# A pooled attention and token/channel mixer on one core: feature-half head, three score bursts, contiguous uT, column-tiled tails

## The chip, the cores and the metric

The kernel runs on 1 core of one Trainium2 chip. The metric is the device time of one execution in microseconds. Shown is the median of the runs with its lowest and highest value.

## What is computed

For 8 batches of 8 heads, 576 positions and 64 features, K and V are averaged over groups of 8 positions (72 pooled keys), attention is taken over the 72 keys, and the result x (8, 576, 512) goes through a token mixer and a channel mixer:

```python
k_p = k.reshape(B, H, Sp, pool, D).mean(axis=3)            # Sp = 72, pool = 8
v_p = v.reshape(B, H, Sp, pool, D).mean(axis=3)
attn = softmax(scale * np.matmul(q, k_p.transpose(0, 1, 3, 2)))
attn_out = np.matmul(attn, v_p)                            # (8, 8, 576, 64)
x = attn_out.transpose(0, 2, 1, 3).reshape(B, S, H * D)    # (8, 576, 512)
h = np.maximum(x.transpose(0, 2, 1) @ w_tok1, 0.0) @ w_tok2  # 576 -> 256 -> 576
u = x + h.transpose(0, 2, 1)
out = u + np.maximum(u @ w_ch1, 0.0) @ w_ch2               # 512 -> 1536 -> 512
```

Inputs and output are float32. The kernel works in bfloat16 with float32 accumulation.

## The kernel before

**Positions.** A batch's 576 positions are cut into 4 chunks of 128 and a tail of 64 (c = 0 to 3 and c = 4). The tails of two batches share one 128-row tile, and all 8 tails are the last MLP unit.

**Order of the work.** Nothing is scheduled automatically: each engine runs its instructions in the order in which the program issues them, and waits for its semaphores at the head of its queue. The order is written out by hand. `HEAD` is a list of steps for batch 0's attention and token mixer (d8 is eight dummy matmuls on a zeroed tile). Then come units 0 to 8: unit n is the channel MLP of batch n (unit 8: of all tails). A unit is a Python generator which yields every two or four matmuls, 45 to 48 times. `PLAN[n]` says which steps of later batches are issued after which yield: "15: 1.K0 1.Q0" issues two steps of batch 1 after yield 15 of that unit.

**Steps of a batch.** `lk lq lv` start the loads, by DMAs on POOL's queue that cast to bfloat16. `K0 K1 V0 V1` pool on POOL by three adds a half (L164 to L170), `k0 .. v1` do the same on VectorE, `kp vpool` on TensorE by eight accumulating identity matmuls. `kpT` transposes the pooled keys, `Q0 Q1` transpose q on VectorE (L262). `s0` to `s3` are score bursts: 8 matmuls with 32 contraction rows each on four row tiles of TensorE (L273), then two exponentials on ACT (L279). `av` is attention times V with the sum in a 65th column (L311), divided on VectorE (L323, L329). `at0 at1` are the first token product (L357) with its relu, `u` the second (L372) with the residual added on VectorE (L373). For the tails, w_tok2's last 64 columns lie in a zero-padded tile `w_tok2t`, so that two batches' tails add up into one 128-row output by four full matmuls.

**u transposed.** The MLP needs u with features on the partitions. Batches 0 to 3 transpose it on TensorE (`t`, L382) and copy it out on VectorE (L383). Batches 4 to 7 write u to device memory (`M0 M2 M4`, L391), read it back in 32-row pieces (`M`, L398, SP's queue) and transpose 32x32 blocks of 4-byte pairs on VectorE (`T`, L405). Such a uT holds pairs of features side by side, and L467 reads every second element of it.

**The MLP.** Twelve tiles of four matmuls each (L467) and relu on ACT into GT (L471). Unit 0 then does twelve matmuls for each chunk (L494, added out in L500). Units 1 to 8 form the 512x512 second product by seven half-size products (L543, 12 matmuls of 256 columns each). This needs sums of GT tiles on VectorE (`=1a` to `=4b`, L514 and L521) and sums of w_ch2, which are formed once on VectorE at the start of unit 1 (L514). Products go to a PSUM bank as two contiguous halves `ps[:, i]` and are added out on VectorE (`plus`, L564) into s or into o, which SP stores.

**Gates.** `g` makes POOL wait for VectorE's place in its queue (L623, L624).

PSUM has four one-bank buffers (`ps_one`) and two two-bank buffers (`ps_two`, for scores and av).

Of the kernel before, what the change touches and what calls it, by code (L numbers as in the profile page):

```python
# [8 lines left out]
FP32 = mybir.dt.float32  # L9
# [11 lines left out]
HEAD = """c0 c1 d8 q0 d1 q1 d5 kp0 kp1 kt0 d2 o0 e0 kt1 kp2 kp3 o1 e1 kt2 kt3 q2 q3 d2 o2 e2 vpool0 o3 d1 vpool1 e3 d2  # L21
          aw1 av0 av2 d2 av3 at_0 at_2 av4 at_1 at_3 d2 at_4 X0 X1 X2 A0 A1 A2 X3 A3 d3"""
PLAN = [
    {0: "0.u0", 2: "0.u3", 6: "1.k1", 10: "2.lv", 15: "1.K0 1.Q0", 16: "1.kpT 1.Q1 3.lk", 18: "1.V0 1.s1 0.u2", 20: "1.s0", 22: "3.lq 1.v1 1.s2", 24: "2.K0 1.s3", 25: "1.av1", 26: "1.av4", 27: "0.u1 1.av3 1.av2", 30: "2.K1", 32: "1.av0", 36: "1.at0 1.at1", 38: "1.u3 2.V0", 40: "1.u4 1.u0", 44: "3.lv 1.u2 1.u1", 45: "1.t3 1.t0", 46: "1.t1", 47: "1.t2 1.t4"},
    {4: "g", 7: "3.K0 2.kpT", 8: "2.Q1", 9: "2.Q0", 11: "2.s2", 12: "3.Q0", 13: "3.Q1", 14: "2.v1 =3a 2.s0", 15: "4.lv 4.lk", 16: "2.s1", 17: "=1a", 18: "2.s3 =3b", 19: "2.av1", 20: "2.av3", 21: "2.av2", 22: "4.lq", 23: "3.K1 2.av0", 24: "2.av4", 26: "g", 27: "=1b", 28: "3.kpT =2a", 29: "2.at0", 30: "3.s3", 31: "=2b", 32: "=4b 2.at1 =4a", 34: "3.s2", 36: "2.u2", 38: "3.V0", 39: "2.u0 3.s1 2.u3", 40: "2.t2", 41: "2.u1 2.t3", 42: "3.s0 3.V1 2.t0 2.t1"},
    {0: "4.K0 3.av4 5.lk 5.lq", 2: "3.av3", 4: "4.K1", 6: "3.av0", 9: "3.av2", 10: "4.V0 3.av1", 12: "=3b", 14: "3.at0 3.at1", 15: "=3a", 16: "4.kpT", 17: "g", 18: "4.Q0", 19: "=1a 3.u3 4.s1", 20: "4.Q1", 23: "3.u1 4.s3 =2a", 24: "3.u0 =1b 3.u2", 25: "=2b 3.t1", 26: "4.s0", 28: "3.u4 4.s2 =4b", 29: "4.V1", 30: "=4a g", 33: "3.t0", 34: "3.t2 4.av3", 35: "3.t3", 37: "4.av4", 39: "3.t4 4.av1", 41: "5.lv", 42: "4.av2", 44: "4.av0"},
    {0: "5.Q0", 6: "=3a 5.K0", 7: "4.at0 4.at1", 8: "5.K1 5.kpT", 9: "5.V0 4.u1 4.u0 5.Q1", 10: "4.u3 5.s1", 11: "5.V1", 12: "4.u2", 13: "5.s0", 14: "4.M0", 15: "4.M2", 16: "4.M", 17: "5.s3 6.lk", 18: "=3b", 20: "=1a", 21: "g", 22: "5.av3 =2a", 23: "=1b", 24: "6.lq", 25: "=2b", 27: "5.s2 =4a", 28: "=4b", 31: "g 5.av2", 36: "5.av4", 38: "4.T1 4.T3", 39: "4.T2", 40: "4.T0", 43: "5.av0", 44: "5.av1 6.lv"},
    {0: "6.Q0", 6: "=3a 6.K0", 7: "5.at0 5.at1", 8: "6.K1 6.kpT", 9: "6.V0 5.u1 5.u0 6.Q1", 10: "5.u3 6.s1", 11: "6.V1 5.u4", 12: "5.u2", 13: "6.s0", 14: "5.M0", 15: "5.M4 5.M2", 16: "5.M", 17: "6.s3 7.lk", 18: "=3b", 20: "=1a", 21: "g", 22: "6.av3 =2a", 23: "=1b", 24: "7.lq", 25: "=2b", 27: "6.s2 =4a", 28: "=4b", 31: "g 6.av2", 36: "6.av4", 38: "5.T1 5.T3", 39: "5.T2", 40: "5.T0", 43: "6.av0", 44: "6.av1 7.lv 5.T4"},
    {0: "7.Q0", 6: "=3a 7.K0", 7: "6.at0 6.at1", 8: "7.K1 7.kpT", 9: "7.V0 6.u1 6.u0 7.Q1", 10: "6.u3 7.s1", 11: "7.V1", 12: "6.u2", 13: "7.s0", 14: "6.M0", 15: "6.M2", 16: "6.M", 17: "7.s3", 18: "=3b", 20: "=1a", 21: "g", 22: "7.av3 =2a", 23: "=1b", 25: "=2b", 27: "7.s2 =4a", 28: "=4b", 31: "g 7.av2", 36: "7.av4", 38: "6.T1 6.T3", 39: "6.T2", 40: "6.T0", 43: "7.av0", 44: "7.av1"},
    {6: "=3a", 7: "7.at0 7.at1", 9: "7.u1 7.u0", 10: "7.u3", 11: "7.u4", 12: "7.u2", 14: "7.M0", 15: "7.M4 7.M2", 16: "7.M", 18: "=3b", 20: "=1a", 21: "g", 22: "=2a", 23: "=1b", 25: "=2b", 27: "=4a", 28: "=4b", 31: "g", 38: "7.T1 7.T3", 39: "7.T2", 40: "7.T0", 44: "7.T4"},  # L30
    {6: "=3a", 18: "=3b", 20: "=1a", 21: "g", 22: "=2a", 23: "=1b", 25: "=2b", 27: "=4a", 28: "=4b", 31: "g"},
    {14: "=3b", 22: "=1a", 24: "=2a =1b", 25: "=4a", 28: "=2b", 31: "=4b", 34: "=3a"},
# [4 lines left out]
def kernel(  # L37
# [14 lines left out]
    nc = tc.nc  # L52
    B, H, S, D = q.shape
    P = 128
    POOL = 8
    SP = S // POOL
# [3 lines left out]
    SH = S // 2  # L60
# [21 lines left out]
    w_tok2t = singles.tile([P, 2, 2, P], BF16)  # L82
# [8 lines left out]
    u_tails = singles.tile([P, 4, DM], BF16)  # L91
    area = early.tile([P, 6 * 1024], BF16, name="area")
    kpz = area[0:SP, 0:2048].rearrange("j (h e d) -> j h e d", h=H, e=4)
# [9 lines left out]

    def kv(t, src, b, h0, h1, j0=0, j1=SP):
        nc.gpsimd.dma_start(out=t[j0:j1, h0:h1].rearrange("j h i d -> j h (i d)"),
                            in_=src[b, h0:h1].rearrange("h (j i) d -> j h (i d)", i=POOL)[j0:j1])

    def load_kv(b, src, key):
        t = loaded[b, key] = raw.tile([SP, H, POOL, D], BF16, name=key + "r")
        if b == 0:  # L110
            for h0, h1, j0, j1 in ((0, HP, 0, BP), (0, H, BP, SP), (HP, H, 0, BP)):
                kv(t, src, b, h0, h1, j0, j1)
        else:
            kv(t, src, b, 0, H)

    def load_q(b):
        qb = loaded[b, "q"] = raw.tile([P, HP, BR * D + D], BF16, name="qb")
        if b == 0:
            nc.vector.memset(qb[:, :, BR * D:], 0.0)
            nc.gpsimd.dma_start(out=qb[:, 2:HP, 0:BR * D], in_=q_pairs(2, HP))  # L120
        else:
            nc.gpsimd.dma_start(out=quarters(qb), in_=q[b].rearrange("(g l) (j n) d -> (l j) g (n d)", l=4, n=2 * BR))
# [8 lines left out]
    def load_tok():  # L131
        nc.gpsimd.dma_start(out=f2, in_=moe_w_tok2.rearrange("(c p) n -> p c n", p=P))
# [9 lines left out]
    def permute_tok2():  # L142
        src = f2.rearrange("t m (p r) -> t m r p", r=BR)
        dst = w_tok2.rearrange("t m (r p) -> t m r p", p=BP)
        for m in range(2):
            nc.gpsimd.tensor_copy(out=dst[:, m], in_=src[:, m])
        for half in range(2):
            nc.gpsimd.tensor_copy(out=w_tok2t[:, :, half, half * BP:(half + 1) * BP], in_=w_tok2[:, :, 8 * BP:S])

    def load_ch1():  # L150
        for g in range(3):
            cols = slice(g * 512, (g + 1) * 512)
            nc.gpsimd.dma_start(out=w_ch1[:, :, cols], in_=moe_w_ch1[:, cols].rearrange("(p c) n -> p c n", c=4))
# [17 lines left out]

    tails = {}

    def batch_steps(b):
# [5 lines left out]
        def prepare():  # L180
            kp = kpz if first else att.tile([SP, 2, 2, 4, D // 2], BF16, name="kp")
# [12 lines left out]
        def late(key):  # L194
            if key not in st:
                pool, shape = {"x": (mix, [P, 4, DM]), "u": (mix, [P, 4, DM]), "uT": (mix, [P, 4, 4 * P]),
                               "AT": (att, [P, 2, DM]), "qD": (att, [P, 2, S, 2])}[key]
                st[key] = pool.tile(shape, BF16, name=key)
            return st[key]

        def parts(src):
            return src.rearrange("p (m k) -> p k m", k=4)
# [14 lines left out]
        def kp2(a):  # L217
            def go():
                ps = ps_one.tile([P, 512], FP32, name="p1")
                hs = slice(2 * a, 2 * a + 2)  # L220
                for i in range(POOL):
                    nc.tensor.matmul(out=ps[0:SP, 0:2 * D], lhsT=ident[0:SP, 0:SP], rhs=loaded[b, "k"][:, hs, i, :],
                                     start=(i == 0), stop=(i == POOL - 1))
                view = ps[0:SP, 0:2 * D].rearrange("j (h d) -> j h d", d=D)[:, :, None, :].broadcast_to([SP, 2, 2, D])
                (nc.scalar.copy if a == 1 else nc.vector.tensor_copy)(out=kpz[:, hs, 0:4:3, :], in_=view)
            return go

        def kt2(a):
            def go():
                ps = ps_one.tile([P, 2, 2, SP], BF16, name="p1")  # L230
                for odd in range(2):
                    for hl in range(2):
                        nc.tensor.transpose(out=ps[:, odd, hl, :],
                                            in_=kpz[:, 2 * a + hl, 2 * odd:2 * odd + 2].rearrange("j e d -> j (e d)"),
                                            identity=ident[0:SP, 0:SP])
                nc.vector.tensor_copy(out=kT[:, :, 2 * a * SP:(2 * a + 2) * SP], in_=ps.rearrange("m o h j -> m o (h j)"))
            return go

# [28 lines left out]
        def score4(g, half):  # L267
            def go():
                pss = [ps_two.tile([P, 2, 512], FP32, name="p2") for _ in range(2)]
                for db in range(2):  # L270
                    for l in range(4):
                        quad = slice(l * 32, (l + 1) * 32)
                        nc.tensor.matmul(out=pss[l // 2][0:SP, l % 2, 0:SH], lhsT=st["kD"][quad, g, db, :],  # L273
                                         rhs=st["qD"][quad, g, half * SH:(half + 1) * SH, db],
                                         start=(db == 0), stop=(db == 1), tile_position=(l * 32, 0))
                exv = st["ex"][:, 0:H * S].rearrange("j (h n) -> j h n", h=H)[:, :, half * SH:(half + 1) * SH]
                for a in range(2):
                    h = 4 * g + 2 * a
# [426 lines left out]
```

## Time and profile before

| | |
|---|---|
| median of 3 runs | 276.22 us (275.23 to 276.26) |
| profiled execution | 277.01 us, span from first to last instruction 275.2 us |
| granted TensorE clock | 1.0 |
| instructions | 5195 |
| TensorE (PE) busy | 262.3 us, 95% of the span |
| weight loads (PEld) | 156.8 us, 57% |
| VectorE (DVE) | 192.2 us, 70% |
| ScalarE (ACT) | 113.5 us, 41% |
| GpSimd (POOL) | 144.8 us, 53% |
| DMA | 32.71 MB in 36344 packets |

Busy time is the union of an engine's instructions. Matmuls are pipelined, so that a row's mean duration of one matmul (383 ns for 512 columns) is longer than the distance between two of them. The idle time of an engine which nothing waits for costs nothing.

### The profile page before, as it was taken

The page shows a single profiled execution, that of the slowest core. Times are in us where ns is not written, and L with a number is a line of the kernel's source. Part 1 is how long each engine was busy: PE and PEld are TensorE (multiplying, and loading weights), DVE is VectorE, ACT ScalarE, POOL GpSimd, SP SyncE. Part 2 cuts the span into 40 slices and gives each one's busy share as a digit, 9 for nine tenths or more (in the row PEclk, how much of TensorE's full clock was granted, in tenths as well). Part 3 has the DMA queues.
Part 4 walks back from the last instruction along what each step waited for, and adds up shares of the span by engine and source line. Part 5 has one row for each costly group of instructions (what it writes and reads, how often), then busy time and mean ns, then how long its engine had stood idle before and what let it go on. Part 6 is the DMA issues. An engine that isn't in the chain of part 4 may idle for free.

```text
span 275.2 us, 5195 instructions
## 1 busy us (share of the span) xinstructions
PE 262.3 (95%) x2064; PEld 156.8 (57%) x2092; DVE 192.2 (70%) x378; ACT 113.5 (41%) x200; POOL 144.8 (53%) x138
## 2 busy tenths in 40 slices
PE   8989889989999999999997999999999999999994
PEld 3765335454466654784376436944594477477483
DVE  5455887389999978896586765795595568174273
ACT  2453672107834357306840566046604430621610
POOL 8595693974989996199619971798000000010000
PEclk9999999999999999999999999999999999999999
DMA  7999999928491591065399539972405250402204
GB/s 160 188 202 207 203 204 195 193 69 161 65 173 26 101 206 20 4 97 144 90 168 152 155 69 172 176 169 89 88 2 152 86 107 18 136 2 59 96 0 152
DMA packets 36344, 32.71 MB, mean 119 GB/s; under 512 B 13665, under 2 KB 29921, under 8 KB 36321
## 3 DMA queue, kind: packets, MB, share of 16 engines
q0 software_dynamic: 18672, 17.64, 41.9%
q1 hardware_dynamic: 17376, 14.49, 20.7%
q8 instruction: 16, 0.26, 0.4%
q10 hardware_dynamic: 272, 0.26, 0.3%
q14 instruction: 8, 0.06, 0.1%
HBM read 38.21 MB, written 11.80 MB: 182 GB/s over the span
## 4 chain that ended last, share of the span: by engine, by line
PE 58%; DMA 18%; DVE 14%; POOL 4%; issue 2%; ACT 2%; SPq 1%; DVEq 0%; POOLq 0%; ACTq 0%
PE p L467 23%; PE p L543 18%; DMA v<-mem 7%; PE p L372 5%; DMA kr<-in_k_dram 5%; PE p L357 5%; DVE area L514 4%; DMA mem<-u 3%; DMA area<-in_moe_w_tok_dram 3%; PE p L494 3%; PE p L311 2%; PE p L273 2%; DVE u L373 1%; DVE x L329 1%; DVE qD L262 1%
## 5 line engine op out<-in xcount | busy, mean ns | idle before, releaser
L471 ACT ACTIVATE GT<-p 128x512 bf16<-128x512 f32 x108 | 64.4, 596 | 98.9 <-PE p L467 58.3
L467 PE MATMUL p<-uT,w_ch 128*128 128x512 bf16 x366 | 91.8, 383 | 3.4 <-DVE uT L405 1.9
L467 PEld LDWEIGHTS <-w_ch 128*128 128x128 bf16 x432 | 39.4, 97 | 49.5 <-issue 6.5
L624 POOL COPY flag<-flag 1x1 f32<-1x1 f32 x14 | 3.5, 247 | 82.2 <-DVE flag L623 82.2
L279 ACT ACTIVATE ex<-p 72x576 bf16<-72x576 f32 x56 | 33.0, 641 | 18.0 <-PE p L273 17.9
L543 PEld LDWEIGHTS <-area 128*128 128x128 bf16 x384 | 36.6, 98 | 5.2 <-issue 0.5
L543 PE MATMUL p<-area,area 128*128 128x256 bf16 x288 | 36.2, 273 | 0.0
L165 POOL TENSOR_TENSOR t<-t 72x512 f32<-72x512 f32 x25 | 34.3, 1372 | 2.0
L373 DVE TENSOR_TENSOR u<-p,x 128x512 bf16<-128x512 f32 x32 | 21.5, 684 | 13.4 <-PE p L372 13.3
L543 PEld LDWEIGHTS <-GT 128*128 128x128 bf16 x288 | 27.1, 98 | 6.2 <-issue 1.4
L164 POOL TENSOR_TENSOR t<-kr 72x1024 f32<-72x1024 bf16 x13 | 27.7, 2129 | 5.0 <-DMA kr<-in_k_dram 4.6
L164 POOL TENSOR_TENSOR t<-vr 72x1024 f32<-72x1024 bf16 x12 | 25.7, 2143 | 0.7
L543 PE MATMUL p<-w_ch,GT 128*128 128x256 bf16 x192 | 23.8, 273 | 0.1
L564 DVE TENSOR_TENSOR o<-p,s 128x512 f32<-128x512 f32 (+1 forms) x32 | 20.6, 664 | 2.6 <-PE p L543 2.5
L521 DVE TENSOR_TENSOR area<-GT 128x768 bf16<-128x768 bf16 x16 | 10.3, 641 | 16.8 <-ACT GT L471 16.7
L329 DVE TENSOR_TENSOR x<-p,den 128x512 bf16<-128x512 f32 x30 | 20.7, 692 | 1.0
L564 DVE TENSOR_TENSOR s<-p,u 128x512 f32<-128x512 f32 x28 | 19.2, 685 | 3.2 <-PE p L543 3.1
L514 DVE TENSOR_TENSOR area<-GT 128x768 bf16<-128x768 bf16 x16 | 12.7, 798 | 9.6 <-ACT GT L471 9.6
L311 PEld LDWEIGHTS <-ex 72*128 72x128 bf16 x320 | 14.9, 98 | 7.1 <-DVE x L329 1.3
L372 PE MATMUL p<-AT,w_tok 128*128 128x512 bf16 x63 | 17.8, 379 | 0.4 <-DVE u L373 0.4
L311 PE MATMUL p<-vp,ex 72*128 72x65 bf16 x320 | 16.8, 194 | 1.1 <-DVE x L329 0.3
L348 ACT ACTIVATE AT<-p 128x512 bf16<-128x512 f32 x15 | 9.0, 597 | 20.8 <-PE p L357 18.1
(102 smaller groups left out, 325.0 us busy)
## 6 DMA issues: line engine op xcount, KB each, us to landing
out_dram<-o SPq DMA_DIRECT2D x33, 256.0 KB, 3.5
kr<-in_k_dram POOLq DMA_DIRECT2D x7, 576.0 KB, 11.1
qb<-in_q_dram POOLq DMA_DIRECT2D x7, 576.0 KB, 12.1
vr<-in_v_dram POOLq DMA_DIRECT2D x7, 576.0 KB, 8.8
w_ch<-in_moe_w_ch_dram POOLq DMA_DIRECT2D x6, 512.0 KB, 13.3
mem<-u SPq DMA_DIRECT2D x8, 256.0 KB, 2.1
v<-mem SPq DMA_DIRECT2D x8, 160.0 KB, 5.1
v<-mem SPq DMA_DIRECT2D x8, 128.0 KB, 5.4
```

Source lines behind the costliest of these rows:

```text
L164: eng.tensor_tensor(out=t4[:, 0:n], in0=t[:, hs, 0:4], in1=t[:, hs, 4:8], op=ALU.add)
L165: eng.tensor_tensor(out=t4[:, 0:n, 0:2], in0=t4[:, 0:n, 0:2], in1=t4[:, 0:n, 2:4], op=ALU.add)
L279: nc.scalar.activation(out=exv[:, h:h + 2], in_=pss[a][0:SP, :, 0:SH], func=AF.Exp, scale=scale)
L311: nc.tensor.matmul(out=halves[h // 4][:, (h % 4) * (D + 1):(h % 4 + 1) * (D + 1)], lhsT=st["ex"][:, h * S + n0:h * S + n0 + P], rhs=st["vp ...
L329: nc.vector.tensor_tensor(out=dst.rearrange("p (a h d) -> p a h d", a=2, d=D), in0=view[:, :, :, 0:D], in1=den[rows, :, :, None].broadcast ...
L372: nc.tensor.matmul(out=ps, lhsT=w, rhs=a, start=(i == 0), stop=(i == len(mms) - 1))
L373: nc.vector.tensor_tensor(out=dst, in0=ps, in1=x, op=ALU.add)
L467: nc.tensor.matmul(out=ps, lhsT=w_ch1[:, kk, m * P:(m + 1) * P], rhs=uT[kk], start=(kk == 0), stop=(kk == 3))
L471: nc.scalar.activation(out=GT[:, m, :], in_=ps, func=AF.Relu)
L514: nc.vector.tensor_tensor(out=out, in0=a, in1=b, op=ALU.subtract)
L543: nc.tensor.matmul(out=ps[i] if split else ps[:, i], lhsT=a(m)[:, i * P:(i + 1) * P], rhs=w(m), start=start and m == 0 and (i == 0 or spli ...
L564: nc.vector.tensor_tensor(out=out[:, i], in0=ps[i] if type(ps) is list else ps[:, i], in1=other[:, i], op=ALU.add)
```

## The change

**Head.** K, V and the weights are loaded in a new order by `L..` steps; w_ch1 comes in four pieces. `a02` and its like (`avh`) make av of two chunks for four heads, `m02` and its like (`ath`) the first token product of a chunk for half of the features, its relu half on ACT and half on VectorE. w_tok2 is permuted on ACT and VectorE instead of POOL. **Scores.** Two bursts of 8x384 columns, one for each four heads, and one of 16x192 for the rest of all heads. **Batch 1** is pooled on TensorE (`kpool`, `vpool`). **K and V loads** are two DMAs each, 64 rows and 8 rows. **Tails.** `w_tok2t` goes; each batch's tail product writes 64 output rows at column position 0 or 64. The tails' transposes go through memory (`M4`, `MT`, `T4`, `T5`). **u and uT.** u holds two chunks interleaved element by element; the pieces read back are 256 elements wide, and the 4-byte pairs are pairs of positions, so that uT is contiguous and GT's columns are taken with step 2 instead (`chunk`). A product writes every second element of its PSUM bank, `ps[:, :, i]`, and `plus` works on pairs. **Weight sums** are eight steps `w0` to `w7` inside unit 0. All plans are rewritten; below are HEAD and, as an example, units 3 and 4.

```diff
-HEAD = """c0 c1 d8 q0 d1 q1 d5 kp0 kp1 kt0 d2 o0 e0 kt1 kp2 kp3 o1 e1 kt2 kt3 q2 q3 d2 o2 e2 vpool0 o3 d1 vpool1 e3 d2
-          aw1 av0 av2 d2 av3 at_0 at_2 av4 at_1 at_3 d2 at_4 X0 X1 X2 A0 A1 A2 X3 A3 d3"""
+HEAD = """LkA LkT LkB Lq LvT LvA LvB Lt1 Lt2 Lv1 Lc1a Lc1b Lk1 Lc1c Lq1 Lc1d Lc2b Lc2a Lc2c d6 d6 prep c0 d1 d3 q0 d4 c1 d4 kp0 q1 kt0 kp1 e0 kt1 kp2 o0 q2 o1 kt2 e1 q3 o2 vpool0 o3 d1 a02 e2 vpool1 a00 e3 d1 m02 m03 a04 m00 a10 p0 X1 m04 a12 X0 m01 m10 p1 a14 m11 m13 m12 A0 X2 m14 A1 X3 A2 A3"""
...
+    {0: "0.u2 0.u3 g 1.vpool1", 2: "2.lk 0.u0", 4: "1.vpool0 2.lq", 7: "1.kpool 1.Q0", 9: "1.kpT 2.lv", 12: "1.s0", 15: "1.Q1", 18: "1.s2", 19: "0.u1", 20: "w4", 21: "w0", 22: "1.s1", 25: "1.av4 w2", 26: "3.lk 3.lq", 27: "1.av3 w1", 29: "1.av0", 30: "2.K0", 31: "1.av1", 32: "1.av2", 33: "2.Q0 w5", 34: "1.at0", 35: "2.K1 1.at1 1.u4", 36: "1.u2", 37: "2.Q1 1.u3", 38: "1.t2", 40: "1.u0", 41: "1.u1 1.t0", 43: "1.t1", 44: "2.kpT", 46: "1.t3", 47: "w7 w3 w6 2.s0"},
...
-    {0: "5.Q0", 6: "=3a 5.K0", 7: "4.at0 4.at1", 8: "5.K1 5.kpT", 9: "5.V0 4.u1 4.u0 5.Q1", 10: "4.u3 5.s1", 11: "5.V1", 12: "4.u2", 13: "5.s0", 14: "4.M0", 15: "4.M2", 16: "4.M", 17: "5.s3 6.lk", 18: "=3b", 20: "=1a", 21: "g", 22: "5.av3 =2a", 23: "=1b", 24: "6.lq", 25: "=2b", 27: "5.s2 =4a", 28: "=4b", 31: "g 5.av2", 36: "5.av4", 38: "4.T1 4.T3", 39: "4.T2", 40: "4.T0", 43: "5.av0", 44: "5.av1 6.lv"},
+    {1: "4.av0 3.T4", 2: "6.lk", 4: "6.lq 5.K1", 6: "4.av3 5.K0", 7: "4.at0", 8: "4.at1 =3a", 11: "5.kpT =3b", 12: "4.u2 5.s0", 13: "5.V0", 15: "4.u3", 16: "5.s1 4.u0", 18: "4.u1", 19: "5.V1", 20: "=1a g", 21: "g", 22: "3.T5 5.av2", 24: "4.M2 =2a =4a g", 26: "5.s2", 28: "4.M0 =1b =2b", 29: "4.M", 30: "4.T1", 31: "g", 32: "=4b", 34: "4.T0", 35: "5.av0", 36: "4.T2 5.av1", 40: "4.T3 5.av3", 44: "6.lv 6.Q1 5.av4"},
...
     def load_kv(b, src, key):
         t = loaded[b, key] = raw.tile([SP, H, POOL, D], BF16, name=key + "r")
...
-            kv(t, src, b, 0, H)
+        kv(t, src, b, 0, H, 0, BP)
+        kv(t, src, b, 0, H, BP, SP)
...
+        def scores(i):
+            def go():
+                pss = [ps_two.tile([P, 2, 512], FP32, name="p2") for _ in range(2)]
+                spans = [(i, 0, 0, S1)] if i < 2 else [(g, g * (S - S1), S1, S) for g in range(2)]
+                for g, o, n0, n1 in spans:
+                    for db in range(2):
+                        for l in range(4):
+                            quad = slice(l * 32, (l + 1) * 32)
+                            nc.tensor.matmul(out=pss[l // 2][0:SP, l % 2, o:o + n1 - n0], lhsT=st["kD"][quad, g, db, :],
+                                             rhs=st["qD"][quad, g, n0:n1, db], start=(db == 0 and o == 0),
+                                             stop=(db == 1), tile_position=(l * 32, 0), skip_group_check=True)
...
-                    mms = [(w_tok2t[:, m, half, :], tails[b // 2, half][:, m, :]) for half in range(2) for m in range(2)]
+                    for m in range(2):
+                        for half in range(2):
+                            nc.tensor.matmul(out=ps[half * BP:(half + 1) * BP], lhsT=w_tok2[:, m, 8 * BP:S],
+                                             rhs=tails[b // 2, half][:, m, :], start=(m == 0), stop=(m == 1),
+                                             tile_position=(0, half * BP), skip_group_check=True)
...
+    def chunk(u, c, a):
+        return a[:, c::2] if "paired" in u else a[:, c * P:(c + 1) * P]
...
-                    nc.tensor.matmul(out=ps[i] if split else ps[:, i], lhsT=a(m)[:, i * P:(i + 1) * P], rhs=w(m),
+                    nc.tensor.matmul(out=ps[i] if split else ps[:, :, i], lhsT=chunk(u, i, a(m)), rhs=w(m),
...
-            return ps_one.tile([P, 2, 256], FP32, name="p1")
+            return ps_one.tile([P, 256, 2], FP32, name="p1")
...
+        def cols_of(o, half):
+            r = o[:, :, half * 256:(half + 1) * 256]
+            return lambda e: r[:, e] if type(e) is int else r.rearrange("p i n -> p n i")
```

## The prediction

> **What bounds the kernel now.** I read the page first, then the busy times by stretch, then TensorE's timeline, its waits, and the chain of waits. The page says TensorE, but its busy time counts overlapped matmuls, so it can't say how much is left to gain.
>
> ```profile
> PE 262.3 (95%) x2064; PEld 156.8 (57%) x2092; DVE 192.2 (70%) x378; ACT 113.5 (41%) x200; POOL 144.8 (53%) x138
> ...
> PE 58%; DMA 18%; DVE 14%; POOL 4%; issue 2%; ACT 2%; SPq 1%; DVEq 0%; POOLq 0%; ACTq 0%
> ```
>
> The kernel is a head (batch 0's attention), units 0 to 7 (the channel MLP of batch n, with attention and token mixing of later batches woven in) and unit 8 (all tails). A unit begins at its first matmul of L467. Busy time by unit:
>
> ```profile
> 0.00:25.20 25.20, 22.89 (x200) 14.48 (x204) 14.01 (x41) 10.54 (x22) 19.11 (x33) 1.00 1.12 187
> 25.20:60.05 34.85, 32.41 (x218) 15.22 (x221) 24.27 (x35) 12.76 (x23) 25.51 (x20) 1.00 1.11 184
> 60.05:92.50 32.45, 30.91 (x277) 17.81 (x280) 31.59 (x56) 17.02 (x30) 26.37 (x22) 1.00 0.57 94
> 92.50:122.80 30.30, 30.02 (x288) 19.26 (x290) 26.11 (x52) 12.92 (x23) 21.46 (x18) 1.00 0.52 91
> ...
> 149.60:179.40 29.80, 28.09 (x234) 16.75 (x234) 20.90 (x46) 12.52 (x22) 20.12 (x18) 1.00 0.77 141
> ```
>
> Columns: stretch, length, then busy time of PE, weight load, DVE, ACT and POOL, granted clock, DMA share, GB/s. Unit 1 has DVE at 31.6 of 32.45 us: there VectorE binds. Elsewhere it is TensorE, and what counts is its spacing:
>
> ```profile
> 78.87 0.59 PE L357 MATMUL p<-x,w_tok 128*128 128x512 bf16 x2
> 79.30 0.38 PE L357 MATMUL p<-xt,w_tok 128*128 128x512 bf16 x1
> 79.51 0.60 PE L543 MATMUL p<-area,area 128*128 128x256 bf16 x4
> 80.04 0.45 PE L273 MATMUL p<-qD,kD 32*72 32x288 bf16 x8
> 80.43 1.05 PE L543 MATMUL p<-area,area 128*128 128x256 bf16 x8
> ```
>
> Two matmuls of 512 columns start 0.43 us apart: 0.2155 each. Of 256 columns it is 0.109 (84 of L543 in 9.17 us of the chain), of 128 it is 0.055, of 65 it is 0.033. The four of L543 should end at 79.95; the score burst starts at 80.04, and 0.39 later the next work starts. So a burst costs 0.48: two groups of four row tiles side by side, 0.24 of stream, and 0.24 around it (0.09 on either side, the rest between groups).
>
> With these prices I count each unit's matmuls into a need. Unit 1: 48 L467 10.35, 84 L543 9.14, 8 bursts 3.8, 10 L357 2.16, 8 L372 1.72, 40 L311 1.28, transposes 1.15: 29.6. Likewise head 19.2, unit 0 31.6, unit 2 29.9, 3 26.7, 4 27.5, 5 26.7, 6 24.2, 7 and 8 19.5 each: 254.4. Lengths less needs are losses: head 6.0, then 3.3, 2.9, 0.4, 0.1, 2.3, 1.1, 0.4, 0.5, and 3.9 for the last adds and stores: 20.8, with the needs 275.2. Only about 11 of them lie in units 0 to 7. TensorE's waits name the largest (total, times, longest):
>
> ```profile
> PE p L467 <- DVE uT L405: 1.9, 2, 1.5
> PE p L213 <- POOL kp L168: 1.7, 1, 1.7
> PE p L467 <- DVE uT L383: 0.7, 1, 0.7
> ```
>
> And on the chain of waits (start, length, what):
>
> ```profile
> 34.34 0.91 POOL kp L168
> ...
> 133.88 2.15 DMA mem<-u
> ...
> 137.94 11.77 DMA v<-mem
> 149.84 1.44 DVE uT L405 x4
> ```
>
> Unit 0 waits for batch 1's keys (landed at 29.0, then pooled on POOL); units 4 and 5 wait for u, sent through memory to be transposed.
>
> **The change part by part.** TensorE's need first.
> - Batch 1's K and V pooling goes to TensorE in unit 0: 8 matmuls of 512 columns and 16 of 256, 1.72 + 1.74 = +3.5.
> - Score bursts: 28 of 8x288 become 14 of 8x384 (0.32 + 0.24) and 7 of 16x192 (0.32 + 0.24 + 0.08 for two more group changes): 13.4 becomes 12.3, -1.1.
> - Tail u: 16 full matmuls of L372 on w_tok2t (3.45) become 16 with 64 output rows, in pairs on two column tiles. No row shows column tiles. If a pair runs side by side as the row tiles do, a tail costs 2 x 0.21 + 0.22 = 0.65, in all 2.6; if not, 4 x (0.86 + 0.19) = 4.2. So -0.85 to +0.75. I take -0.85, from the nearest row, the bursts: there four tiles take one tile's time.
> - Tail transposes (8 of L382) leave, -0.4; two dummies fewer, -0.4.
> - Net +0.7: 255.2. By unit: head 18.8, 35.1, 28.9, 28.6, 27.0, 26.9, 25.8, 25.1, 19.5, 19.5.
>
> [...]
>
> Free by rows: weights taken at every second column (L382's weights stand four apart, and its transposes keep 0.055 spacing); contiguous uT (the paired one already ran at 0.2155).
>
> **VectorE.** In unit 0 it loses the pooling 1.k1 and 1.v1 (L164, L165, L168, L170: 4.5 each) and gains three evacuations (0.69 + 2 x 0.42); the eight weight sums (0.55 each, 4.4) move from unit 1's start into unit 0. Adding up the new order by row means gives 25 us in unit 0, 26 in unit 1 (31.6 before; two qD transposes leave as well) and 27 in unit 2. So unit 1 turns from VectorE-bound into TensorE-bound, 26 under 28.9; unit 2 has 27 under 28.6, tight.
>
> **POOL and DMA.** Each K and V load is issued twice (64 and 8 rows). A 72-row issue took 0.85, an 8-row one 0.61: 0.6 more for each of 14 loads, 8.5 us of POOL's queue; what waits behind is pooling steps. POOL had 144.8 of 275 busy and loses batch 1's pooling (8.7): hidden. Without that cover each is 0.6. To 41 us the DMA engines are saturated (about 200 GB/s) with 7.4 MB, the same bytes in another order. By that rate V1 lands near 20, K1 near 26.5, Q1 31.5, the halves of w_ch1 needed for m=4 and m=8 at 29.5 and 34, w_ch2 at 41.5. The new plan needs them near 26, 32, 32, 32, 36.5 and 40 to 44: about 2 us of room, and the 1.7 us wait for kp goes. w_ch1 in quarters adds 0.6 (512-byte packets of w_tok took 60 ns against 98 for 1 KB): hidden by that room. The spill reads 512-byte instead of 256-byte pieces and starts as soon as u is written, with the transposes at steps 30 to 40; next unit's K and Q loads now precede it. So the 1.5 and 0.5 us waits of units 4 and 5 go.
>
> **Head.** 24 dummies now stand before kp0 (14 before): 12 at the unwarmed 0.43 end at 6.3, the other 12 and q0 at 9.2, while K was used at 7.65. So K's chain begins 1.6 later. Then av and at come in half-width pieces and a02 needs only heads 0 to 3. Following the chain by row durations (evacuation 0.42, reciprocal 0.2 and multiply 0.69, two score/av buffers) gives a02 at 16.2 (av at 16.3 before), VectorE full from 16.7 to 24, unit 0 at 25.3: loss 6.5. In this stretch the w_tok2 permutation comes to ACT and VectorE (1.24 each on POOL before); by the 576-element cast, 0.46, and that 1.24 it takes VectorE 0.5 to 1.2, I take 0.6, one element per 1.04 ns as in L329. Each 0.1 more delays unit 0 by 0.1.
>
> **Losses I expect.** Unit 0, 1.6: 1.av4 follows s1 by three half tiles (1.3) but needs two exponentials of 0.8 each (0.5); 1.u4 follows 1.at1 at once and its second half waits for a 0.6 activation (0.5), and behind it on TensorE stand 1.u2 and the next products; the last av before at0 and the last uT copy 0.3 each. Units 1 and 2, 0.9 each, between the 0.4 that unit 2 lost with VectorE at 86% and the 2.9 of unit 1 at 97%. Units 3 to 7, 0.4 each, as 6 and 7 now. End unchanged, 3.9. In all 15.8: span 255.2 + 15.8 = 271.0. The profiled execution took 277.01 for a span of 275.2, and the median of the runs, 276.22, is 0.8 below it; so 271.0 + 1.0 = 272.0.
>
> **Rivals.**
> *Stalls come back.* VectorE's 78 us in units 0 to 2 stand against 92.6 of TensorE, in unit 2 94%, and a sum on GT took 0.80 beside busy POOL against 0.55 alone (L514's groups). If units 0 to 2 lose 6.6 as now instead of 3.4 and the spill is late again (2.2), span 276.4, time 277; with one of the two, 274 to 275. Against it: the weight sums and two poolings have left the tight stretch.
> *The output adds get slow.* o is now written column pair by column pair, two rows 2 KB apart in turn. L262 writes 4-byte words 8 bytes apart at 1.31 ns an element, no slower than L405's packed 1.61; no row goes further. From no cost to twice (0.53 more on 4 adds a unit): units 1 and 2 would become VectorE-bound (28.1 and 29.2) and every unit's end later, about 4 us: 276.
> *Products into every second PSUM column.* The products of units 1 to 7 (84 each) and 36 of unit 8 now write 4-byte words 8 bytes apart: 624 matmuls. No matmul of before writes so. Below: nothing, as stride 2 costs nothing where qD is read (288 columns in 0.12). Above: half rate, 0.109 more each, 68 us: 340. From 0.007 us each on it eats the whole 4.2 us gain. For the forecast I take nothing, since stride 2 is free in every row that has it, if only on reads.
> [...]
> *Nothing waits.* All losses of units 0 to 7 at 0.1 to 0.2, as unit 3 now: span 255.2 + 6.5 + 3.9 + 1.0, time 267.6.
>
> **How the numbers follow.** Forecast 0.62 (267 to 274.8), stalls back 0.16 (274 to 278, a quarter of it still faster), slow adds 0.07 (275 to 279), PSUM 0.11 (slower), nothing waits 0.04. A measurement of this kernel can tell about 0.5% from no change, 274.8 to 277.6. Faster 0.62 + 0.04 + 0.04 = 0.70; same 0.10 from the middle of the second and third; slower 0.11 + 0.09 = 0.20. The range 266 to 279 leaves out the PSUM case and the ends of the others.
>
> **What would show it.** Right: product matmuls still 0.109 apart; burst groups at 0.56; unit 1 about 30 us with VectorE near 26; no wait for kp or for uT from memory; unit 0 starting near 25.3 and lasting 36 to 37. Wrong: product spacing over 0.116, L564's successor over 0.7 for o, unit 0 over 38 or the head over 26.5.

## The result, and the profile after

The changed kernel takes 338.69 us (median of 4 runs, 338.25 to 339.09) against 276.24 for the kernel before on the same chip: 1.227 times, 95% interval 1.223 to 1.230. The forecast was 272.0. The profiled span is 336.9 us. The later experiments ran in three groups, each on one chip, where the kernel before took medians of 276.6 to 278.7 us with a mean granted clock of 0.982 to 1.0, so each ratio below is against the runs of the kernel before in its own group, fast runs alone.

From the page of the changed kernel, the busy times and the chain of waits:

```profile
span 336.9 us, 5265 instructions
...
PE 328.6 (98%) x2108; PEld 184.0 (55%) x2108; DVE 200.1 (59%) x385; ACT 110.8 (33%) x179; POOL 140.3 (42%) x152
...
PE 93%; DVE 4%; issue 1%; ACT 1%
```

TensorE's busy time grew by 66 us, the other engines' shares fell, and the share of DMA in the chain (18% before) is gone. So the kernel doesn't wait more; TensorE works longer. Units 0, 1 and 4, each cut at its first weight load of L497 (stretch, length, busy PE, PEld, DVE, ACT, POOL, clock, DMA share, GB/s):

```profile
25.50:63.90 38.40, 36.43 (x256) 17.35 (x255) 24.56 (x48) 12.77 (x21) 23.25 (x22) 1.00 0.96 169
63.90:101.70 37.80, 37.80 (x277) 21.45 (x274) 25.80 (x46) 16.35 (x26) 26.82 (x25) 1.00 0.63 103
...
176.00:211.70 35.70, 35.70 (x227) 19.51 (x225) 21.69 (x42) 12.21 (x20) 18.53 (x18) 1.00 0.52 108
```

Unit 0, which still ends in twelve plain matmuls a chunk, is 1.7 us over the forecast of 36.7; units 1 and 4, with the seven half-size products, are 8.0 and 8.4 us over it. TensorE's timeline in unit 1 says what changed (start, length, what), and the cost groups of the page say it for the kernel:

```profile
86.01 0.54 PE L285 MATMUL p<-qD,kD 32*72 32x192 bf16 x16
86.48 1.90 PE L583 MATMUL p<-area,area 128*128 128x256 bf16 x8
```

```profile
L583 PE MATMUL p<-area,area 128*128 128x256 bf16 x288 | 64.1, 407 | 0.0
L624 DVE TENSOR_TENSOR o<-p,s 128x512 f32<-128x512 f32 (+1 forms) x32 | 31.5, 1026 | 27.4 <-PE p L583 27.4
```

Eight products of 256 columns took 1.05 us before and take 1.90 now: their starts lie 0.216 us apart in the trace, where they lay 0.109. It is so in all units, also in 1 to 3, where the weights (`chunk`) stay contiguous; so the second-column weights aren't it. 624 products by 0.107 are 66.7 us, and 336.9 less 66.7 is 270.2, beside the forecast span of 271.0. The waits of TensorE that are left are small:

```profile
PE p L216 <- DVE kp L246: 1.6, 1, 1.6
...
PE p L457 <- DVE w_tok L145: 0.6, 1, 0.6
```

### The profile page after: what moved, and what is told of

Same layout as the page of the kernel before. It is cut to its first block, busy times and chain, and to the rows that moved or that the text cites. A ratio compares the mean times of both kernels' runs of the same rounds, so it can differ in the third digit from the quotient of the medians.

```text
span 336.9 us, 5265 instructions
## 1 busy us (share of the span) xinstructions
PE 328.6 (98%) x2108; PEld 184.0 (55%) x2108; DVE 200.1 (59%) x385; ACT 110.8 (33%) x179; POOL 140.3 (42%) x152
## 4 chain that ended last, share of the span: by engine, by line
PE 93%; DVE 4%; issue 1%; ACT 1%
PE p L583 41%; PE p L497 27%; PE p L377 5%; PE p L398 4%; PE p L285 3%; PE p L363 2%; PE p L675 2%; PE p L527 2%; PE p L254 1%; DVE o L624 1%; PE p L406 1%; DVE kp L246 1%; PE p L306 1%; PE p L393 1%; DVE x L368 1%
## 5 line engine op out<-in xcount | busy, mean ns | idle before, releaser
L497 PE MATMUL p<-uT,w_ch 128*128 128x512 bf16 x384 | 93.8, 380 | 0.0
L497 PEld LDWEIGHTS <-w_ch 128*128 128x128 bf16 x432 | 40.3, 99 | 45.2 <-issue 2.4
L583 PEld LDWEIGHTS <-area 128*128 128x128 bf16 x384 | 50.2, 133 | 26.6 <-issue 0.6
L583 PE MATMUL p<-area,area 128*128 128x256 bf16 x288 | 64.1, 407 | 0.0
L583 PEld LDWEIGHTS <-GT 128*128 128x128 bf16 x288 | 36.9, 130 | 21.4 <-issue 1.3
L624 DVE TENSOR_TENSOR o<-p,s 128x512 f32<-128x512 f32 (+1 forms) x32 | 31.5, 1026 | 27.4 <-PE p L583 27.4
L583 PE MATMUL p<-w_ch,GT 128*128 128x256 bf16 x192 | 42.3, 409 | 0.0
L294 ACT ACTIVATE ex<-p 72x768 bf16<-72x768 f32 x42 | 31.5, 802 | 31.1 <-PE p L285 31.1
L161 POOL TENSOR_TENSOR t<-t 72x512 f32<-72x512 f32 x23 | 30.3, 1319 | 1.8
L160 POOL TENSOR_TENSOR t<-kr 72x1024 f32<-72x1024 bf16 x12 | 25.7, 2143 | 6.4 <-DMA kr<-in_k_dram 5.8
L160 POOL TENSOR_TENSOR t<-vr 72x1024 f32<-72x1024 bf16 x11 | 23.4, 2123 | 0.8 <-DMA vr<-in_v_dram 0.2
L583 PE MATMUL p<-w_ch,area 128*128 128x256 bf16 x96 | 22.8, 419 | 0.0
L583 PE MATMUL p<-area,GT 128*128 128x256 bf16 x96 | 21.5, 400 | 0.1
L553 DVE TENSOR_TENSOR area<-GT 128x768 bf16<-128x768 bf16 x16 | 11.6, 727 | 10.7 <-ACT GT L501 10.7
```

The source lines that it names most:

```text
L160: eng.tensor_tensor(out=t4[:, 0:n], in0=t[:, hs, 0:4], in1=t[:, hs, 4:8], op=ALU.add)
L161: eng.tensor_tensor(out=t4[:, 0:n, 0:2], in0=t4[:, 0:n, 0:2], in1=t4[:, 0:n, 2:4], op=ALU.add)
L294: nc.scalar.activation(out=dst, in_=src, func=AF.Exp, scale=scale)
L497: nc.tensor.matmul(out=ps, lhsT=w_ch1[:, kk, m * P:(m + 1) * P], rhs=uT[kk], start=(kk == 0), stop=(kk == 3))
L583: nc.tensor.matmul(out=ps[i] if split else ps[:, :, i], lhsT=chunk(u, i, a(m)), rhs=w(m), start=start and m == 0 and (i == 0 or split), st ...
L624: nc.vector.tensor_tensor(out=aps[0], in0=aps[1], in1=aps[2], op=ALU.add)
```

## The experiments

Theory: a matmul that writes every second PSUM word runs at half rate, and the rest of the change is worth what the prediction says, span about 271. Rivals: the contiguous uT or the second-column weights slow the products; or the o adds (1.03 us) hold the banks. The diffs below are shortened to the arguments that change.

**The stride alone, added to the kernel before.**

```diff
-    out=ps[i] if split else ps[:, i]          # bank [P, 2, 256]
+    out=ps[i] if split else ps[:, :, i]       # bank [P, 256, 2]
-    in0=ps[:, i]
+    in0=ps.rearrange("p n i -> p i n")[:, i]
```

> The kernel before with one part of the change: products write every second 4-byte word of their bank, and the adds read them so; all else is as before. PSUM theory: 624 matmuls at 0.107 more, 66.7 us less what stalls of 11 us in units 0 to 7 give back: 335 to 343. Rival: within 3 us of 276.

Measured: 342.84 us, ratio 1.233 (1.220 to 1.245). Its products, on the page (mean 273 ns before):

```profile
L543 PE MATMUL p<-area,area 128*128 128x256 bf16 x288 | 64.9, 407 | 0.0
```

One edit to the kernel before costs 65.6 us of span (340.8 against 275.2; by the medians 64.2), with no other part of the change in it. Its output adds, which read the strided bank one half at a time and write contiguous rows, take 0.67 us, as before (0.66): reading PSUM with that step cost VectorE nothing here.

**The stride taken away from the changed kernel.** In `product`, `bank`, `keep`, `part`, `residual` and `cols_of` the order is half by half (where u is stored in pairs, from unit 4 on, the s adds are two of 256 columns each):

```diff
-    out=ps[i] if split else ps[:, :, i]
+    out=ps[i] if split else ps[:, i]
-    return ps_one.tile([P, 256, 2], FP32, name="p1")
+    return ps_one.tile([P, 2, 256], FP32, name="p1")
```

> The changed kernel with one part undone: products write contiguous halves of their PSUM bank again, and s and o are added in that order. PSUM theory (a matmul whose 4-byte outputs lie 8 bytes apart runs at half rate, 0.216 instead of 0.109 for 256 columns): 624 matmuls lose 0.107 each, 66.7 us, so the span goes from 336.9 to 270.2 and the time to about 272 (269 to 275); products 0.109 apart. Rival (the rest of the product loop, that is weights taken with step 2, interleaved u, or slower adds holding the banks): units 4 to 7 keep 0.2 apart and the time stays above 300.

Measured: 282.06 us, ratio 1.013 (1.005 to 1.021), span 280.0. The products are 0.109 apart again, 57 us are back and the o adds take 0.67. But 9 us of the forecast are missing: the spacing that was expected of the products came, the time of 269 to 275 did not.

**Contiguous banks, but o still added pair by pair.** As the one before, with the o add writing the two rows of o in turn; in units 1 to 3 s is then stored in another order than the o adds read it, so that part of the result differs, with the same amount of work.

> As e1_contiguous, but the output adds keep the order of the change: two rows of o, 2 KB apart, in turn, read from the two halves in turn. PSUM theory: products 0.109 apart as in e1_contiguous; the adds into o take 1.0 us or more instead of 0.69, 1.4 us more VectorE a unit, and the time is 0 to 4 us above e1_contiguous. Rival (the slow adds hold the PSUM banks and are the loss): the time stays above 300.

Measured: 287.63 us, ratio 1.032 (1.024 to 1.040). The o add takes 1.055 us (0.666 without), and the version takes 5.6 us more. Unit 1 lasts 29.3 us, as without (29.1), with VectorE busy 25.5; most of the loss lies in unit 4 (32.3 against 27.8), where TensorE waits 2.6 us for an s add that stands behind a transpose waiting for u from memory, and a stretch at half clock comes with it. How the slower adds lead there was not followed. So the rival of the slow output adds was real in size (0 to 0.53 was given, 0.36 to 0.39 is it), but VectorE doesn't become the limit of unit 1, as that rival had it; in the changed kernel itself the slow products hide the adds.

**A ruler for PSUM writes.** The kernel before with rows of eight equal matmuls at the end of the head (and two cold rows at its start), each row with another pattern of output words.

```diff
+    out = (bank[:, 0:256],                                                 # z0 contiguous
+           bank.rearrange("p (n e) -> p e n", e=2)[:, 0],                  # z1 every second word
+           bank.rearrange("p (n e r) -> p e n r", e=2, r=2)[:, 0],         # z2 two in, two out
+           bank.rearrange("p (n e r) -> p e n r", e=2, r=4)[:, 0],         # z3 four in, four out
+           bank.rearrange("p (n e) -> p e n", e=4)[:, 0],                  # z4 every fourth word, 128 columns
+           bank.rearrange("p (n e) -> p e n", e=4)[:, 0:2])[int(s[1:])]    # z5 every fourth, in two passes
```

> The kernel before with its eight first dummies replaced by 8 + 8 matmuls of 256 columns, contiguous and then with step 2, at the unwarmed clock, and before unit 0 a ruler of 8 matmuls each: contiguous, step 2, two words in and two out, four in and four out, step 4 (128 columns), two in and two out counted from another view, contiguous. [...] If any gap in the pattern slows: two in and two out also takes more than 0.15. If each strided word costs two cycles of TensorE's own clock: unwarmed, step 2 takes 0.427.

The run took 281.15 us with the added matmuls; what counts are the distances from start to start in its trace, us:

```
columns, words written               later   first 3.8 us
256 contiguous (z0, first and last)  0.109   0.213
256 every second word (z1)           0.216   0.426 (one distance)
256 two in, two out (z2)             0.109
256 four in, four out (z3)           0.109
128 every fourth word (z4)           0.109
256 every fourth word, twice (z5)    0.216
```

What counts is pairs: a pair of neighbouring words and a lone word take the same 0.85 ns (0.109 / 128, 0.216 / 256). The distance to the next pair or word, here up to four words, is free. The order counts, not the set of words: z5 writes the very words of z2, but every fourth one first and their neighbours in a second pass, and takes twice as long, 0.216 for 0.109. In the kernel's first 3.8 us, ahead of the first record of its clock, both patterns take twice as long, which reads as half clock (where the record has 0.50, at 117.27 in the contiguous version, eight contiguous products take 1.89 in place of 1.05); the factor of 2 stays. So of the two theories on record the last holds there (0.427 expected), and the other, that any gap slows, is refuted by z2 and z3 (0.109).

**Where the missing 9 us went.** Against the forecast unit 0 lasts 2.9 us longer in the contiguous version, unit 2 3.2 and unit 3 4.6; all else is 1.8 shorter. The waits of TensorE there (the expectations count each about 0.17 us longer, by the distance from start to start), then VectorE's and GpSimd's timelines at the first of them:

```profile
PE p L583 <- DVE area L553: 2.2, 1, 2.2
PE p L583 <- DVE area L546: 1.7, 1, 1.7
```

```profile
110.53 0.56 DVE L546 TENSOR_TENSOR area<-area,GT 128x768 bf16<-128x768 bf16 x1
111.13 2.37 DVE L546 TENSOR_TENSOR area<-GT,area 128x768 bf16<-128x768 bf16 x1
...
114.02 1.86 DVE L553 TENSOR_TENSOR area<-GT 128x768 bf16<-128x768 bf16 x1
```

```profile
111.31 1.25 POOL L104 DMA_DIRECT2D kr<-in_k_dram  x2
112.54 0.75 POOL L114 DMA_DIRECT2D qb<-in_q_dram  x1
113.30 2.16 POOL L160 TENSOR_TENSOR t<-kr 72x1024 f32<-72x1024 bf16 x1
115.54 1.46 POOL L161 TENSOR_TENSOR t<-t 72x512 f32<-72x512 f32 x1
```

The same sum takes 0.56 in one place and 1.86 to 3.54 (at 148.3) in others. The one that began at 114.02 ends at 115.88, 0.42 after L160's add has ended and 0.34 into L161's. That is the mark of a held sum: 15 of the 16 sums that take over 0.6 end 0.41 to 0.43 us after the end of an add of GpSimd's. Over the whole trace, the 45 sums that lie beside no add and no DMA issue of GpSimd's take 0.52 to 0.56, and the 16 beside its adds alone 1.18 on the mean. VectorE's operations on PSUM (the x multiplies, 0.69) take the same beside them. After each of the two waits comes a second loss (same columns as above, clock third from the end):

```profile
113.15:116.57 3.42, 1.15 (x8) 0.55 (x7) 3.42 (x5) 0.13 (x1) 3.34 (x3) 1.00 1.20 193
116.57:119.98 3.41, 3.24 (x28) 2.50 (x28) 3.34 (x6) 0.00 (x0) 3.25 (x3) 0.50 1.27 201
```

For one stretch of 3.4 us TensorE has half its clock, about 1.7 us lost, in unit 2 and again in unit 3.

**The evacuation of the pooled K.** L246 took 2.41 us where 0.69 was taken; the contiguous version with one edit, in one instruction:

```diff
-    out=st["kp"].rearrange("j g e l d -> j g (l d) e"), in_=ps[0:SP].rearrange("j (g n e) -> j g n e", g=2, e=2)
+    out=st["kp"].rearrange("j g e l d -> j g e (l d)"), in_=ps[0:SP].rearrange("j (g n e) -> j g e n", g=2, e=2)
```

> The changed kernel with contiguous halves in PSUM (as in e1_contiguous) and one edit more: the evacuation of batch 1's pooled K (72x512, line 246) writes its feature halves one after the other instead of alternating 256 bytes apart. Theory A (the far-alternating writes are what makes it long, 2.41 us): it takes 0.7 to 0.9 us, the wait of TensorE for it in unit 0 (1.8 us at 33.2) is gone, and the span falls from 280.0 to about 278. Theory B (its length is the PSUM read or the 32-byte input step, which stay): 2.4 us again and no change. Units 2 and 3 keep their waits of 2.4 and 1.9 us and their slow stretch of the clock in both theories.

```profile
L246 DVE CAST kp<-p x1: 687/687/687, 33.7 to 33.7; 72x512 bf16<-72x512 f32 x1
```

Measured: 280.45 us, ratio 1.011 (1.002 to 1.019), span 278.5. Writing alternately to places 256 bytes apart made it 3.5 times as long. The read of PSUM changes too, from word after word to every second word; that step cost VectorE nothing in the first experiment (0.67 with it, 0.66 without), so it can't be the gain. The wait is gone.

**GpSimd kept off the sums.** The same, with two edits of the plan:

```diff
 unit 2:
-  24: "=1a 5.lv =2a =4a", 26: "=1b 4.s2 3.t2", 27: "=2b =4b"
+  24: "=1a =2a =4a", 26: "=1b 4.s2 3.t2", 27: "=2b =4b g 5.lv"
 unit 3:
-  31: "g", 32: "=4b"
+  32: "=4b g"
```

> e5_kp_near with two edits of the step plan: in unit 2 the load of batch 5's V goes behind the last sums, with a gate for GpSimd ahead of it; in unit 3 the gate in front of the last sum goes behind it. Theory A (VectorE's sums on bf16 halves are held as long as GpSimd issues its DMAs or adds: 2.37, 1.87 and 3.54 us at 111, 114 and 148 instead of 0.55; TensorE waits for them 2.4 and 1.9+1.2 us, and each wait is followed by one 3.4-us stretch at half clock that costs another 1.7): these sums take about 0.55, the waits and both slow stretches go, units 2 and 3 fall from 32.8 and 32.0 to about 28.7 and 27.2, the span to 269 to 271. Theory B (the sums are late because VectorE has too much to do in these units): the sums are shorter but the waits move to the next VectorE result, and the span stays above 275. Theory C (the slow clock comes by itself, not from the waits): units 2 and 3 gain the waits alone and one or two slow stretches stay, the span about 273.

Measured: 274.12 us, ratio 0.988 (0.981 to 0.995), span 272.4, clock 1.0 throughout. The span fell by 6.1 us and ends 1.4 above the range of theory A. VectorE's timeline at the same two sums, and units 2 and 3:

```profile
110.52 0.56 DVE L546 TENSOR_TENSOR area<-GT,area 128x768 bf16<-128x768 bf16 x1
...
111.60 0.55 DVE L553 TENSOR_TENSOR area<-GT 128x768 bf16<-128x768 bf16 x1
```

```profile
92.20:121.60 29.40, 28.84 (x268) 18.09 (x265) 24.29 (x51) 12.43 (x20) 23.05 (x22) 1.00 0.60 119
121.60:149.00 27.40, 27.39 (x244) 16.91 (x242) 21.23 (x46) 12.43 (x20) 17.37 (x18) 1.00 0.46 115
```

Against the version before it unit 2 fell from 32.8 to 29.4 and unit 3 from 31.6 to 27.4, with nothing taken out of VectorE's work, and both stretches at half clock went: the causes of theory A. GpSimd's adds do hold these sums of VectorE's, by the 0.41 to 0.43 us above, and not its operations on PSUM (the x multiplies, 0.69 beside them as elsewhere). Why these and not those is not shown. Whether the issue of a DMA holds them too is open: eight sums beside issues alone took 0.54 to 0.56, but the one of 2.37 began amid issues, 2.2 us ahead of the next add. A held sum costs nothing where TensorE doesn't need it next: this version still has some of up to 2.5 us.

**The same for the head and unit 0.** The second half of the w_tok2 permutation moves to ScalarE, and the weight sum w5 moves six steps earlier.

```diff
-    (nc.vector.tensor_copy if m else nc.scalar.copy)(out=dst[:, m], in_=src[:, m])
+    nc.scalar.copy(out=dst[:, m], in_=src[:, m])
 unit 0:
-  27: "1.av3 w1", ... 33: "2.Q0 w5"
+  27: "1.av3 w1 w5", ... 33: "2.Q0"
```

> e6_pool_gated with two edits more: the second half of the permute of w_tok2 goes from VectorE (1.11 us, TensorE waits 1.0 us at 20.7) to ScalarE behind its first half, and the weight sum w5 of unit 0 goes six steps earlier, ahead of GpSimd's pooling of batch 2 (it took 1.85 us there, and TensorE waited 0.9 + 0.7 us for the x behind it). Theory A: unit 0 starts about 0.8 earlier, and unit 0 is 1.3 to 1.6 shorter, the span 266.5 to 269. Rival: ScalarE's AT copies come later by the 1.24 us of the second permute and the head stays as it was; then only unit 0 gains, and the span falls by 1.5.

Measured: 275.77 us, ratio 0.993 (0.989 to 0.997), span 273.9: 1.5 longer than the version before it. The head gained: unit 0 begins at 23.3 and no wait for w_tok is left (the five versions with the head as it was began at 24.1 to 25.8, so that only the wait of 0.6 to 0.8 is surely this edit's). Unit 0 lost: its weight sums now met GpSimd's first pooling of batch 2. VectorE's timeline, and what came after:

```profile
44.76 3.67 DVE L546 TENSOR_TENSOR area<-w_ch,area 128x768 bf16<-128x768 bf16 x2
```

```profile
44.87:48.28 3.41, 1.25 (x13) 0.52 (x11) 3.41 (x2) 0.00 (x0) 3.25 (x3) 1.00 1.20 203
48.28:51.70 3.42, 2.38 (x13) 1.18 (x14) 3.32 (x9) 0.00 (x0) 3.26 (x3) 0.50 1.25 207
51.70:55.11 3.41, 3.41 (x9) 1.21 (x8) 0.96 (x2) 0.60 (x1) 3.25 (x3) 0.50 0.81 145
```

TensorE waited 3.2 us, to 49.3, for the x behind them, and two stretches of half clock came, 6.8 us in all; the expectation of the next run speaks of one. Both theories on record missed: the sum moved into the pooling instead of ahead of it.

**A gate behind w5.**

```diff
-  27: "1.av3 w1 w5"
+  27: "1.av3 w1 w5 g"
```

> e7_head_u0 with one step more: a gate for GpSimd behind the weight sum w5 of unit 0, so that its pooling of batch 2 starts only when w1 and w5 are done. In e7 both sums fell together on that pooling (2.13 and 1.61 us at 44.8 and 46.8), TensorE waited 3.4 us at 45.7 for the x behind them and one slow stretch of the clock followed. Theory A (sums held by GpSimd, slow stretch from the wait): both sums take 0.55, no wait over 1 us and no slow stretch are left, unit 0 falls from 42.35 to 36.5 to 37.5, the span to 267.5 to 269.5 and the time to 269 to 271.5. Rival: the pooling, about 1.5 us later, is late for batch 2's scores (kT, then the bursts at the end of unit 0), TensorE waits there instead, and the span stays at 271 or more.

```profile
44.84 1.01 DVE L546 TENSOR_TENSOR area<-w_ch,area 128x768 bf16<-128x768 bf16 x2
```

Measured: 272.17 us, ratio 0.987 (0.981 to 0.993), span 269.7, the clock at 1.0 throughout. The same two sums take 1.01 us in place of 3.67 and unit 0 lasts 37.0 in place of 42.35: the causes of theory A, with span and time just above its ranges (269.5 and 271.5). After the first wait for the dummies' operands no wait of TensorE is over 0.6:

```profile
PE p L681 <- DVE area L735: 1.2, 1, 1.2
PE p L406 <- DVE uT L407: 0.6, 1, 0.6
```

This version has all parts of the change but the stride, the pairwise order and the kp order, and besides them the moved steps and gates. It takes 1.3% less than the kernel before (0.7 to 1.9%).

## Why the prediction was wrong

**The step that failed** is in the PSUM rival: "For the forecast I take nothing, since stride 2 is free in every row that has it, if only on reads." The term was 0 and measured 0.107 us on each of 624 matmuls, 66.7 us. Upper bound and sum (340) were right; the choice between the ends was not. The rows it was taken from are TensorE reading SBUF (qD, uT, weights), another memory and another direction, and with one end at +68 us and a gain of 4 at stake, 0.11 was too small a chance. The range left that case out.

**Terms whose size was off**, hidden behind the slow products until these were mended:
- The kp evacuation of batch 1: 0.69 taken from a packed row, 2.41 measured. So the kp wait did not go, it changed its cause (1.7 us before, 1.6 now).
- The o adds: 0 taken, 0.36 to 0.39 measured on each; 5.6 us in the version that uncovers them. The price in the rival (0.53, 4 us) was about right, its way to it (VectorE as the limit of units 1 and 2) is not what unit 1 shows.
- The w_tok2 permutation on VectorE: 0.6 taken, 1.1 measured; TensorE waits 0.6 to 0.8.
- Losses in units 2 and 3, half clock included: 1.3 taken, 9.2 measured in the contiguous version (4.2 and 5.0). The rival "stalls come back" had the right place (sums beside GpSimd, unit 2 tight), but priced a held sum at 0.80 from a group mean. A mean hid the two sorts: 0.52 to 0.56, or 0.65 to 3.54. Half clock behind a wait was in no term. In the changed kernel the same sums are held as long (2.36 and 1.87 us at 120.6 and 123.5) and nothing waits, since twelve products beside them last 2.6 us instead of 1.3.

**Steps that held.** Unit 0's first matmul came at 25.75 (25.3 forecast). Bursts of 8x384 cost 0.46 to the next start and 0.09 ahead (0.56 forecast), those of 16x192 the same 0.56 (0.64 forecast). The column tiles of a tail do run side by side: two matmuls of L393 start 4 ns apart in the last version, and a tail's four take 0.55 to the next start and 0.1 ahead (0.65 forecast), so the dearer case beside that term, 4.2 for the four tails, isn't seen. No wait for a uT from memory is left; contiguous uT and second-column weights cost nothing: L497's matmuls start 0.216 apart in every unit of the changed kernel (on the paired uT of the kernel before, from unit 4 on, 0.225, not the 0.2155 that was taken), and with second-column weights still in it the contiguous version has its products back at 0.109. With stride and held sums away, the sum of needs and losses stands: from unit 0's first matmul to the end 245.7 us were forecast and 246.1 measured in the last version; units 1 to 4 there last 29.5, 29.3, 27.6, 27.7 (29.8, 29.5, 27.4, 27.3 forecast). That the total comes so near is in part luck, since GpSimd's gates and the moved steps were not in the forecast. What of the 1.3% is the change and what those isn't separated; the kernel before has held sums too (2.4 and 2.5 us in unit 1). A reading in the prediction is off without changing its sum: from unit 1 on its units are cut at the first weight load of L467, not at the first matmul (unit 1 at 60.05; the matmul came at 60.94), so waits of 0.7 and 1.5 us count to units 1 and 4, which begin with them.

## What to carry to other kernels

Look at the innermost step of what TensorE writes before anything else: in the ruler two neighbouring words at a time, then a gap, ran at full rate (0.109 us for 256 columns), and word by word took twice as long (0.216). When a fix makes one engine faster, look for the waits that its slowness covered: here 9 us of them came up behind 67. Keep GpSimd's adds away from VectorE's sums whose result TensorE wants next (here 0.52 to 0.56 us alone, 1.18 on the mean beside adds), and read the single durations, since a group's mean mixes free and held ones.

## What was not expected of the hardware

- A wait of TensorE can cost more than its length, and what counts is not the single wait. In all ten traces the recorded stretches of one clock last whole multiples of 3.413 us (in the contiguous version 33, 1, 10, 1 and 36 of them), so in these traces the clock goes by windows on a fixed grid. Eight windows at full clock in which TensorE was idle for 1.88 to 2.28 us in all were each followed by one at half clock, some 1.7 us more; windows with up to 1.65 us idle (the kernel before, at 33.8) were not. In these traces the edge lies between. A wait of 1.6 us, half of it inside the window, brought it together with one of 1.1 (1.88 in all); waits of 1.4 and 1.1 us in two neighbouring windows (1.47 and 0.97 idle) did not. After the wait of 3.2 us a second window at half clock followed a first one with only 1.0 us idle; why is open.
- VectorE's write to two places 256 bytes apart in turn (2-byte words) takes 3.5 times as long as the packed one, 2.41 for 0.69 us; two places 2 KB apart with 4-byte words, 1.07 for 0.68 (the o add of the changed kernel and of the contiguous version).
